# Alternating side banks, eight output products a slot and turned first layers in a fused attention and gated feed-forward kernel

## Chip, cores, metric

The kernel runs on one core of a Trainium2 chip. The metric is device time in microseconds, the median of several executions. PE is TensorE, ACT is ScalarE, DVE is VectorE, POOL is GpSimd, SP is SyncE.

## The reference, cut to what matters

```python
h   = softmax(scale * inducing @ x.T) @ x          # 32 inducing rows, per batch; B = 4, N = 12416, C = 128
a   = softmax(scale * x @ h.T) @ h                 # per token; 49664 tokens in all
g, v = a @ w_gate, a @ w_val                       # 128 -> 1536 each
out = a + sigmoid(a @ w_res) * ((gelu(g) * v) @ w_out)
```

Per token only 32 softmax weights `r` are needed: `a = r @ h`, so `g = r @ (h @ w_gate)`. The first layers `hg = h @ w_gate` and `hv = h @ w_val` are 32 x 1536 per batch; the kernel holds them, halved, in four copies along the partitions. Matmuls go in row-tiled pairs: one takes partitions 0 to 63 and the other 64 to 127, so each sums over two of the copies (a pair of 512 columns takes 0.39 us in the traces).

## The kernel before

The main loop goes by *slots*. A slot computes 1024 columns: a gate pair on PE, Gelu on ACT, a value pair on PE and a product `u` on DVE. Six slots make a *group* of 512 tokens and 12 chunks of 128 features. Everything else is put into a slot's *window*, which is issued after the slot's value pair: the 48 output products of a group (`mms`), two mixes of the group (gate, residual), and work for the next batch. In the traces PE's rows follow the order of the code (slot 5 of the changed kernel: value pair at 745.44, mix at 745.66, products at 745.97).

```python
ps_gv = ... tile_pool(name="psgv", bufs=3, PSUM)    # 3 x 2 banks, gate and value pairs in turn
ps_f  = ... tile_pool(name="psf", bufs=1, PSUM)     # output sums of a group
ps_m  = ... tile_pool(name="psm", bufs=1, PSUM)     # mixes, accumulation, small work
...
def first_layer(b, parts, engs):
    bank = wide_bank()
    ...     # matmuls of 512 columns: all four copies at once, h.T stationary
            act.activation(dst[:, c0:c1], bank[:, o0:o], AC.Copy, bias=0.0, scale=0.5)
...
for gi in range(ngrp):                              # f: first slot of the group
        at(f + 4, lg.gate)                          # mix with hr, then tanh on ACT
        at(f + 6, lg.residual)                      # mix with ha, then a copy on ACT
        for i, n in enumerate((10, 10, 10, 9, 9)):
            at(f + 3 + i, lambda lg=lg, n=n: lg.mms(n))
        at(f + 7, lg.end)                           # DVE: (tanh + 1) * sums; POOL: + residual; store
...
# next batch, per batch: group g, slot p
bg(13 + i, 2, lambda: accumulate(nb, j0, j1, True, True))   # i = 0..4
bg(18, 2, lambda: finish_h(nb)); bg(19, 2, lambda: turn_h(nb))
bg(20, 2, first_layer hg)                           # 1024 columns, one ACT copy
bg(22, 2, first_layer hv); bg(23, 2, first_layer the rest, two copies)
bg(22, 5, lambda: res_layer(nb))
# bursts of exponentials (another ACT table) after slot 2 of groups 12 and 21
```

The trace shows a table load of 1.28 us on ACT before the first exponential of a burst and again before the next Gelu (`ACT_TABLE_LOAD`, 14 in the kernel before, 1283 ns each). Gelus run ahead of the value pairs by a *lead* of up to four slots; a burst sets it to one, and it grows by one in every other group. I number slots by position in the loop: slots 2, 3, 4, 5, then 0 and 1 of the next six, belong to one group's products. Slot 2 has none.

The softmax here doesn't subtract the row's maximum and nothing guards it: scores larger than these inputs give would overflow.

## Time and profile before

| | before |
|---|---|
| median, 4 runs | 865.85 us (864.67 to 866.56) |
| busy DVE, PE, ACT | 92%, 91%, 85% |
| ordinary group, from one closing DVE operation to the next | 7.74 us |
| the two groups after the second burst (22 and 23) | 11.19 + 9.28, 11.31 + 9.28, 8.88 + 9.28 us in batches 1 to 3 |

The closing operation `th<-th,ffn` comes once a group, so differences of its start times are group lengths: the simplest way to compare two kernels of this kind place by place. Groups are counted from 0 in each batch; a *lead-growth* group is one in which the lead grows by one, so that it holds seven Gelus. The lines of the page, the ordinary group and the waits of the first layers stand in the prediction. This is PE in the timeline of an accumulation group, slot 2 (start, length, engine, line; idle time before it in brackets):

```profile
163.94 0.39 PE L289 MATMUL gv<-rt,hv 64*128 64x512 f16 x2
...
164.26 0.25 PE L165 MATMUL ms<-hi,e 128*32 128x128 f16 x4
...
165.52 0.39 PE L289 MATMUL gv<-rt,hv 64*128 64x512 f16 x2 [0.18 <-ACT ge L298]
```

The accumulation starts at 164.26, and even after it PE waits 0.18 us for ACT before it may issue slot 3's value pair: in the empty slot it lies beside a wait. The sums over a stretch in the first batch (us, busy by engine, granted clock, DMA share):

```profile
226.00:234.00 8.00, 5.97 (x91) 3.97 (x88) 7.86 (x12) 6.10 (x8) 1.90 (x1) 0.99 0.18 35
234.00:241.00 7.00, 6.14 (x38) 3.06 (x37) 4.86 (x5) 3.69 (x5) 4.97 (x3) 0.53 0.29 73
```

After eight microseconds in which PE was busy 5.97, the granted clock is on average 0.53 for 7 us (0.50 from 233.8 to 240.6, which I call a half-clock stretch), and DVE works 4.86 of 7.

### The profile page before, as it was taken

The numbers are of one execution on the slowest core, as the hardware profiler recorded it, in microseconds if no ns is written. First come the engines' busy times: TensorE is split into PE (matmuls) and PEld (weight loads), VectorE is DVE, ScalarE is ACT, GpSimd is POOL, SyncE is SP. The second block draws the span as 40 slices with busy tenths as digits, with TensorE's granted clock in tenths as the row PEclk, the third lists the DMA queues.
The fourth block names the chain that finished last, engine by engine and source line by source line (L and its number), as shares of the span: only waits on it lengthen the run. The fifth ranks groups of instructions, "written<-read, shape, count | busy, mean of one in ns | idle before, by whom it ended". The sixth has DMA issues, their size and how long they took to land.

```text
span 863.7 us, 23212 instructions
## 1 busy us (share of the span) xinstructions
PE 789.5 (91%) x9548; PEld 473.8 (55%) x9548; DVE 798.7 (92%) x784; ACT 734.9 (85%) x870; POOL 347.6 (40%) x304
## 2 busy tenths in 40 slices
PE   5889999999889999999988999999988899999997
PEld 4545556555545555656554555565554555555554
DVE  8689999999989999899988999989998999999997
ACT  5588988989878888898978888989888898889885
POOL 2429885112266776112145787411225711111111
PEclk9599999999999999999989999999999999999999
DMA  8337875010147776101034677410114411100111
GB/s 308 108 70 155 199 171 142 27 38 26 38 98 139 185 184 138 41 26 38 26 69 95 165 181 171 104 39 26 38 34 92 101 39 39 38 32 32 38 38 40
DMA packets 114185, 77.04 MB, mean 89 GB/s; under 512 B 92416, under 2 KB 95136, under 8 KB 114080
## 3 DMA queue, kind: packets, MB, share of 16 engines
q1 hardware_dynamic: 111792, 73.14, 33.5%
q10 hardware_dynamic: 2288, 2.43, 1.0%
q8 instruction: 74, 1.21, 0.6%
q14 instruction: 31, 0.25, 0.1%
HBM read 27.87 MB, written 25.43 MB: 62 GB/s over the span
## 4 chain that ended last, share of the span: by engine, by line
PE 68%; DVE 14%; ACT 11%; issue 5%; DMA 1%; POOL 1%; DVEq 0%; POOLq 0%; SPq 0%; ACTq 0%
PE ffn L328 31%; PE gv L289 30%; ACT ge L298 10%; DVE u L305 9%; PE ms L337 4%; DVE lo L116 1%; DVE hi L114 1%; DVE z L242 1%; DVE th L356 1%; ACT hg L215 1%; DMA ge<-in_moe_w_out_dram 1%; POOL wO L417 0%; PE gv L212 0%; DMA rt<-a 0%; DMA xf<-in_x_dram 0%
## 5 line engine op out<-in xcount | busy, mean ns | idle before, releaser
L305 DVE TENSOR_TENSOR u<-ge,gv 128x1024 bf16<-128x1024 f32 x584 | 693.0, 1214 | 48.4 <-PE gv L289 24.2
L298 ACT ACTIVATE ge<-gv 128x1024 f32<-128x1024 f32 x584 | 586.0, 1021 | 88.4 <-PE gv L289 63.6
L328 PE MATMUL ffn<-wO,u 128*128 128x128 bf16 x4656 | 346.8, 221 | 0.6 <-DVE th L356 0.6
L328 PEld LDWEIGHTS <-u 128*128 128x128 bf16 x4656 | 263.7, 98 | 113.9 <-issue 93.0
L359 POOL TENSOR_TENSOR at<-at,th 128x512 f32<-128x512 f32 (+1 forms) x100 | 124.0, 1240 | 428.3 <-ACT ge L298 361.3
L289 PE MATMUL gv<-rt,hv 64*128 64x512 f16 x1152 | 224.1, 380 | 35.6 <-ACT ge L298 22.7
L289 PE MATMUL gv<-rt,hg 64*128 64x512 f16 x1152 | 225.3, 387 | 8.5 <-ACT ge L298 3.1
L289 PEld LDWEIGHTS <-hv 64*128 64x128 bf16 x1200 | 97.0, 94 | 110.5 <-issue 106.3
L289 PEld LDWEIGHTS <-hg 64*128 64x128 bf16 x1200 | 63.1, 93 | 92.1 <-issue 40.9
L256 POOL TENSOR_TENSOR a<-e,z 128x1024 f16<-128x1024 f32 (+2 forms) x50 | 91.2, 1833 | 27.2 <-DMA rt<-a 14.2
L116 POOL TENSOR_TENSOR lo<-xf,hi 128x1024 f16<-128x1024 f32 x36 | 76.8, 2135 | 0.3
L337 PEld LDWEIGHTS <-rt 64*128 64x128 f16 x768 | 57.6, 94 | 30.8 <-issue 3.6
L356 DVE SCALAR_TENSOR_TENSOR th<-th,ffn 128x512 f32<-128x512 f32 (+1 forms) x100 | 66.5, 665 | 1.0 <-PE ffn L328 1.0
L345 ACT ACTIVATE th<-ms 128x512 f32<-128x512 f32 (+1 forms) x100 | 58.0, 580 | 2.4 <-PE ms L337 2.4
L351 ACT ACTIVATE at<-ms 128x512 f32<-128x512 f32 (+1 forms) x100 | 58.0, 580 | 1.9 <-PE ms L337 1.8
L114 POOL CAST hi<-xf 128x1024 f16<-128x1024 f32 x36 | 37.3, 1037 | 29.5 <-DMA xf<-in_x_dram 19.5
L337 PE MATMUL ms<-ha,rt 64*128 64x128 f16 x384 | 36.6, 215 | 1.1 <-DVE hr L225 1.1
L337 PE MATMUL ms<-hr,rt 64*128 64x128 f16 x384 | 37.5, 219 | 0.0
L141 PEld LDWEIGHTS <-xt 128*128 128x128 f16 x768 | 24.3, 99 | 7.0 <-issue 6.4
L132 ACT ACTIVATE xt<-gv 128x1024 f16<-128x1024 f16 x12 | 12.3, 1024 | 13.3 <-PE gv L131 13.3
L131 PE MATMUL gv<-identF,hi 128*128 128x128 f16 x96 | 11.0, 285 | 9.0 <-DVE hi L114 8.8
L235 ACT ACTIVATE e<-gv 128x1024 f32<-128x1024 f32 (+2 forms) x13 | 11.9, 959 | 7.9 <-PE gv L141 7.8
(88 smaller groups left out, 261.3 us busy)
## 6 DMA issues: line engine op xcount, KB each, us to landing
out_dram<-at SPq DMA_DIRECT2D x96, 256.0 KB, 2.0
xf<-in_x_dram SPq DMA_DIRECT2D x42, 512.0 KB, 4.3
ge<-in_x_dram SPq DMA_DIRECT2D x6, 512.0 KB, 6.1
rt<-a SPq DMA_TRANSPOSE x49, 3.1
xt<-hi SPq DMA_TRANSPOSE x36, 3.2
ge<-in_moe_w_gate_dram ACTq DMA_DIRECT2D x1, 512.0 KB, 4.5
ge<-in_moe_w_val_dram ACTq DMA_DIRECT2D x1, 512.0 KB, 5.6
ge<-in_moe_w_out_dram ACTq DMA_DIRECT2D x1, 512.0 KB, 4.5
```

The source lines that it names most:

```text
L114: e_hi.tensor_copy(hi[:, :w, :], xf[:, :w, :])
L116: e_lo.tensor_tensor(lo[:, :w, :P], xf[:, :w, :], hi[:, :w, :], AL.subtract)
L256: po.tensor_tensor(a2[:, :n], ev[:, o:o + n, :].unsqueeze(2).to_broadcast([P, n, Q, M]), z[:, 1, o:o + n].unsqueeze(2).unsqueeze(3).to_bro ...
L289: pe.matmul(v[:, c * tw:(c + 1) * tw], weights[b][r, (c0 + c) * P:(c0 + c + 1) * P], rt[r, :], start=True, stop=True)
L298: act.activation(ge[:, :n], v, AC.Gelu, bias=0.0, scale=1.0)
L305: ve.tensor_tensor(u[:, :n], ge_t.pop((gi, si)), v, AL.mult)
L328: pe.matmul(self.ffn[:, k, :], u_t[self.gi, si][:, o:o + P], wO[:, fc, :], start=first, stop=not self.todo, skip_group_check=True)
L337: pe.matmul(bank[:, k * P:(k + 1) * P], rt_t[self.b, self.k][r, self.j0 + k, :], h[r, :], start=True, stop=True)
L345: act.activation(self.th[:, :self.tw], bank[:, :self.tw], AC.Tanh, bias=0.0, scale=0.5)
L351: act.activation(self.at[:, :self.tw], bank[:, :self.tw], AC.Copy, bias=0.0, scale=1.0)
L356: ve.scalar_tensor_tensor(self.th[:, :tw], self.th[:, :tw], 1.0, self.ffn.rearrange("p k c -> p (k c)")[:, :tw], AL.add, AL.mult)
L359: po.tensor_tensor(self.at[:, :tw], self.at[:, :tw], self.th[:, :tw], AL.add)
```

## The change

Its intent: to spread the products evenly over all six slots (which needs a second bank for the sums, since slot 2 belongs to a time when the last group's sums are still read), to put the mixes at the start of a window, and to make the first layers cheaper for PE's banks and ACT. The diff, cut to its core (schedule conditions, renamed pools and the final drain are cut):

```diff
-    ps_f = ... bufs=1     ps_m = ... bufs=1
+    ps_2 = two pools "ps0", "ps1", bufs=1 each
+    def side_bank(group):
+        return ps_2[group % 2].tile([P, TOK], FP32, name="sb", tag="sb")
     def misc_bank():
-        return ps_m.tile([P, TOK], FP32, name="ms", tag="ms")
+        return side_bank(parity[0] + 1)             # parity: the group of the window
...
+    def first_layer_t(b):                           # 24 matmuls of 32 columns, weights stationary
+        bank = wide_bank()
+        for o, w in ((0, wG), (TOK, wV)):
+            for c in range(FCH):
+                pe.matmul(bank[:, o + c * M:o + (c + 1) * M], w[:, c * P:(c + 1) * P],
+                          ht_t[b][:, 0:M], start=True, stop=True)
+        act.activation(hgt_t[b], ..., AC.Copy, bias=0.0, scale=0.5)   # 768 columns
+    def spread(b, i):                               # POOL copies fourfold, DMA turns it
+        po.tensor_copy(a2, src.unsqueeze(2).to_broadcast([P, n, Q, M]))
+        ... sy.dma_start_transpose(...)
...
-            at(f + 4, lg.gate)
-            at(f + 6, lg.residual)
-            for i, n in enumerate((10, 10, 10, 9, 9)):
-                at(f + 3 + i, lambda lg=lg, n=n: lg.mms(n))
-            at(f + 7, lg.end)
+            for i in range(6):
+                at(f + 2 + i, lambda lg=lg: lg.mms(8))
+            at(f + 5, lg.gate, START)
+            at(f + 6, lg.residual, START)
+            at(f + 7, lg.end, LATE)
...
-                bg(13 + i, 2, ... accumulate ...)
-            bg(18, 2, finish_h)  bg(19, 2, turn_h)
+                bg(13 + i, 3, ... accumulate ..., START)
+            bg(18, 3, finish_h, START)  bg(19, 3, turn_h, START)
+            bg(20, 3, first_layer_t, START)
+            for i in range(3):
+                bg(20, 5 + i, lambda i=i: spread(nb, i))
-            bg(20, 2, first_layer hg)  bg(22, 2, hv)  bg(23, 2, the rest)
-            bg(22, 5, lambda: res_layer(nb))
+            bg(23, 3, lambda: res_layer(nb), START)
```

The output buffers `u` go from 8 to 7. Both mixes of a group now use the other group's bank, one after the other.

More of the change, by code (lines that the diff above doesn't have):

```diff
@@ L71 @@
     p_ge = ctx.enter_context(tc.tile_pool(name="gelu", bufs=6))
-    p_u = ctx.enter_context(tc.tile_pool(name="up", bufs=8))
+    p_u = ctx.enter_context(tc.tile_pool(name="up", bufs=7))
     p_fin = ctx.enter_context(tc.tile_pool(name="fin", bufs=2))
     ps_gv = ctx.enter_context(tc.tile_pool(name="psgv", bufs=3, space=bass.MemoryType.PSUM))
-    ps_f = ctx.enter_context(tc.tile_pool(name="psf", bufs=1, space=bass.MemoryType.PSUM))
-    ps_m = ctx.enter_context(tc.tile_pool(name="psm", bufs=1, space=bass.MemoryType.PSUM))
+    ps_2 = [ctx.enter_context(tc.tile_pool(name=f"ps{i}", bufs=1, space=bass.MemoryType.PSUM))
+            for i in range(2)]
     ctx.enter_context(tc.manual_schedule())
+    parity = [0]
+    def side_bank(group):
+        return ps_2[group % 2].tile([P, TOK], FP32, name="sb", tag="sb")
     def misc_bank():
-        return ps_m.tile([P, TOK], FP32, name="ms", tag="ms")
+        return side_bank(parity[0] + 1)
     def wide_bank():
@@ L217, in first_layer @@
                 ve.tensor_scalar(dst[:, c0:c1], bank[:, o0:o], 0.5, None, op0=AL.mult)
+    hgt_t = {}
+    def first_layer_t(b):
[4 more added lines that the diff above has]
+                          ht_t[b][:, 0:M], start=True, stop=True)
+        hgt_t[b] = p_h.tile([P, 2, FCH * M], BF16, name="hgt", tag="hgt", bufs=1)
+        act.activation(hgt_t[b], bank.rearrange("p (s n) -> p s n", s=2)[:, :, :FCH * M],
+                       AC.Copy, bias=0.0, scale=0.5)
+    def spread(b, i):
+        n = 2 * FCH // 3
+        src = hgt_t[b].rearrange("p s (c m) -> p (s c) m", m=M)[:, i * n:(i + 1) * n, :]
+        a2 = p_sm.tile([P, PRE, Q, M], BF16, name="a2", tag="a2")
+        po.tensor_copy(a2, src.unsqueeze(2).to_broadcast([P, n, Q, M]))
+        for dst, c0, c1 in ((hg_t[b], 0, FCH), (hv_t[b], FCH, 2 * FCH)):
+            lo, hi = max(c0, i * n), min(c1, (i + 1) * n)
+            if lo < hi:
+                sy.dma_start_transpose(
+                    dst.rearrange("p (c f) -> p c f", f=P)[:, lo - c0:hi - c0, :],
+                    a2[:, lo - i * n:hi - i * n].rearrange("p c q m -> p (c q m)"))
     def res_layer(b):
@@ L323, in mms @@
                 if first:
-                    self.ffn = ps_f.tile([P, TOK // P, P], FP32, name="ffn", tag="ffn")
+                    self.ffn = side_bank(self.gi).rearrange("p (k c) -> p k c", c=P)
                 si, c = divmod(fc, per)
@@ L333, in mix @@
         def mix(self, h):
-            bank = misc_bank()
+            bank = side_bank(self.gi + 1)
             r = slice(0, 2 * M)
@@ L451 @@
         norm_b(0, j0, j1, exp_b(0, j0, j1))
-    warm = ps_f.tile([P, TOK // P, P], FP32, name="ffn", tag="ffn")
+    warm = side_bank(0)
     for i in range(10):
-        pe.matmul(warm.rearrange("p k c -> p (k c)"), wG[:, :P], wG[:, :TOK],
-                  start=True, stop=True)
+        pe.matmul(warm, wG[:, :P], wG[:, :TOK], start=True, stop=True)
     flat = [(gi, si) for gi in range(ngrp) for si in range(len(groups[gi][4]))]
@@ L469, with at @@
     LEAD = 4
-    def at(i, f):
-        windows.setdefault(i, []).append(f)
+    START, MIDDLE, END, LATE = range(4)
+    def at(i, f, where=MIDDLE):
+        windows.setdefault(i, []).append((where, f))
     for gi in range(ngrp):
@@ L477 @@
         if len(groups[gi][4]) == 6:
-            at(f + 4, lg.gate)
-            at(f + 6, lg.residual)
-            for i, n in enumerate((10, 10, 10, 9, 9)):
-                at(f + 3 + i, lambda lg=lg, n=n: lg.mms(n))
-            at(f + 7, lg.end)
-        else:
-            at(f + 1, lg.gate)
-            at(f + 3, lg.residual)
+            for i in range(6):
[3 more added lines that the diff above has]
+            at(f + 7, lg.end, LATE)
+        else:
+            at(f + 2, lg.gate, START)
             at(f + 3, lambda lg=lg: lg.mms(len(lg.todo)))
-            at(f + 3, lg.end)
+            at(f + 3, lg.residual, START)
+            at(f + 3, lg.end, LATE)
     def plan(b):
@@ L491, in plan, with bg @@
         i0 = first[b * gpb]
-        def bg(g, p, f):
-            at(i0 + 6 * g + p, f)
+        def bg(g, p, f, where=END):
+            at(i0 + 6 * g + p, f, where)
         if b == 0:
@@ L510, in plan @@
             for i, (j0, j1) in enumerate(zip(cuts, cuts[1:])):
-                bg(13 + i, 2, lambda j0=j0, j1=j1: accumulate(nb, j0, j1, True, True))
-            bg(18, 2, lambda: finish_h(nb))
-            bg(19, 2, lambda: turn_h(nb))
+                bg(13 + i, 3, lambda j0=j0, j1=j1: accumulate(nb, j0, j1, True, True), START)
+            bg(18, 3, lambda: finish_h(nb), START)
+            bg(19, 3, lambda: turn_h(nb), START)
+            bg(20, 3, lambda: first_layer_t(nb), START)
+            for i in range(3):
+                bg(20, 5 + i, lambda i=i: spread(nb, i))
             e2s = []
@@ L522, in plan @@
                 bg(21, 3 + i, lambda: norm_b(nb, *e2s.pop(0)))
-            bg(20, 2, lambda: first_layer(nb, [(hg_t[nb], wG, 0, cw)], [act]))
-            bg(22, 2, lambda: first_layer(nb, [(hv_t[nb], wV, 0, cw)], [act]))
-            bg(23, 2, lambda: first_layer(
-                nb, [(hg_t[nb], wG, cw, F), (hv_t[nb], wV, cw, F)], [act, act]))
-            bg(22, 5, lambda: res_layer(nb))
+            bg(23, 3, lambda: res_layer(nb), START)
             for i in range(ntile):
                 j = 6 * 21 + 5 + (5 * i) // 2
-                at(i0 + j, lambda i=i: weights_b(nb, i))
+                at(i0 + j, lambda i=i: weights_b(nb, i), END)
     for b in range(B):
@@ L546, in window_next @@
     def window_next():
-        for f in windows.pop(sent["w"], []):
+        i = sent["w"]
+        if i < nflat:
+            parity[0] = flat[i][0]
+        for _, f in sorted(windows.pop(i, []), key=lambda e: e[0]):
             f()
@@ L575 @@
     assert not bursts
-    for i in sorted(windows):
-        for f in windows[i]:
-            f()
+    while windows:
+        window_next()
 _INS = ['x', 'inducing', 'moe_w_gate', 'moe_w_val', 'moe_w_out', 'moe_w_res']
```

## The prediction

> **What bounds the kernel now.** I read the engine table first, then the costliest groups, then the timeline of one ordinary group late in the kernel, then the places where VectorE (DVE) waits. From the page:
>
> ```profile
> PE 789.5 (91%) x9548; PEld 473.8 (55%) x9548; DVE 798.7 (92%) x784; ACT 734.9 (85%) x870; POOL 347.6 (40%) x304
> ...
> L305 DVE TENSOR_TENSOR u<-ge,gv 128x1024 bf16<-128x1024 f32 x584 | 693.0, 1214 | 48.4 <-PE gv L289 24.2
> L298 ACT ACTIVATE ge<-gv 128x1024 f32<-128x1024 f32 x584 | 586.0, 1021 | 88.4 <-PE gv L289 63.6
> ```
>
> Three engines are near full, so the balance inside a slot decides. A slot is one gate pair, one value pair, a Gelu and a DVE product `u`; six slots make a group of 512 tokens. DVE looks saturated, but its rows hide small waits. These are DVE rows of the timeline (start, length, group):
>
> ```profile
> 146.06 2.35 DVE L305 TENSOR_TENSOR u<-ge,gv 128x1024 bf16<-128x1024 f32 x2
> ...
> 743.07 0.68 DVE L356 SCALAR_TENSOR_TENSOR th<-th,ffn 128x512 f32<-128x512 f32 x1
> 743.67 7.23 DVE L305 TENSOR_TENSOR u<-ge,gv 128x1024 bf16<-128x1024 f32 x6
> ...
> 750.81 0.68 DVE L356 SCALAR_TENSOR_TENSOR th<-th,ffn 128x512 f32<-128x512 f32 x1
> ```
>
> Two `u` with nothing between take 2.35 us, so one follows another after 2.35 - 1.22 = 1.13 us. Six would take 5 x 1.13 + 1.22 = 6.87; they take 7.23. So each ordinary group loses about 0.36 us that no idle column shows. Its period is 750.81 - 743.07 = 7.74 us, against a DVE floor of 6 x 1.13 + 0.60 = 7.38 (0.60 is 743.67 - 743.07). The next rows, of PE and ACT in the same group, show where the loss is:
>
> ```profile
> 745.34 1.02 ACT L298 ACTIVATE ge<-gv 128x1024 f32<-128x1024 f32 x1 [0.60 <-PE gv L289]
> 745.61 0.73 PE L328 MATMUL ffn<-wO,u 128*128 128x128 bf16 x10
> 746.26 0.59 ACT L345 ACTIVATE th<-ms 128x512 f32<-128x512 f32 x1
> 746.28 0.39 PE L289 MATMUL gv<-rt,hg 64*128 64x512 f16 x2
> ...
> 747.82 0.39 PE L289 MATMUL gv<-rt,hv 64*128 64x512 f16 x2
> 748.03 0.38 PE L337 MATMUL ms<-ha,rt 64*128 64x128 f16 x4
> 748.35 0.68 PE L328 MATMUL ffn<-wO,u 128*128 128x128 bf16 x9
> ...
> 748.95 0.39 PE L289 MATMUL gv<-rt,hg 64*128 64x512 f16 x2
> 749.18 0.38 PE L289 MATMUL gv<-rt,hv 64*128 64x512 f16 x2
> ```
>
> PE from one value pair to the next, 747.82 to 749.18, needs 1.36 us, more than DVE's 1.13; the following `u` starts 0.49 after the second. The other part comes from ACT: tanh stands between two Gelus, the value pair at 747.82 waits for the bank that the second one reads. Slot 2, by contrast, has no output products, and there PE waits 0.27 us for ACT.
>
> The larger waits are in the second half of each of the first three batches, where the next batch's first layer is made:
>
> ```profile
> 237.13 1.22 DVE L305 TENSOR_TENSOR u<-ge,gv 128x1024 bf16<-128x1024 f32 x1 [0.71 <-PE gv L289]
> 239.29 1.22 DVE L305 TENSOR_TENSOR u<-ge,gv 128x1024 bf16<-128x1024 f32 x1 [0.93 <-PE gv L289]
> ...
> 249.02 1.22 DVE L305 TENSOR_TENSOR u<-ge,gv 128x1024 bf16<-128x1024 f32 x1 [1.37 <-ACT hv L215]
> ```
>
> [...] from 234 to 241 us the granted clock is 0.53 here, after the scores' burst, and that is in the waits of 0.71 and 0.93.
>
> **The change part by part.** *Products.* PE lengths from the rows: value pair to first product 0.31 (749.18 to 749.49), with a mix between 0.53 (747.82 to 748.35); ten products to the next gate pair 0.67, nine 0.60, so eight about 0.55; gate to value pair 0.22. Before: slots 3 and 5 take 0.31 + 0.67 + 0.22 = 1.20, slot 4 (gate mix) 1.42, slot 0 (residual mix) 1.36, slot 1 1.13. After: 1.08 each, and 1.30 in the two mix slots, 5 and 0. All plain slots fall under DVE's 1.13. But the two mix slots now follow each other and share one bank, so the residual mix waits until tanh has read the gate mix.
>
> After, steady state: a value pair can run no earlier than about 0.6 before its `u` starts, since its bank goes `u` end, gate pair, Gelu, value pair (0.06 + 0.45 + 1.02 + 0.06 + 0.49 past a `u` end, against 2 x 1.13). That is 0.1 to 0.2 of slack. Slots 5 and 0 use 2 x (1.30 - 1.13) = 0.34 of it. The mix's wait for tanh: Gelu of slot 5 starts about 0.45 after its gate pair, tanh 0.92 later, its end with the release 0.65 later, 2.0 in all; PE itself reaches the mix 0.22 + 1.30 + 0.22 = 1.75 after the gate pair, or 1.9 where the value pair waits for a Gelu. So another 0.05 to 0.2. Estimate of the group's loss: 0.34 - 0.15 + 0.1 = 0.29, against 0.36. Gain 0.07 a group; some 50 ordinary groups: -4 us.
>
> *Groups where the lead of Gelus grows* (nine; 8.63 us each, with waits of 0.35 and 0.20): the 0.35 is two Gelus in one slot and stays; the PE chain from slot 3 to slot 1 shrinks from 1.20 + 1.42 + 1.20 + 1.36 = 5.18 to 1.08 x 2 + 1.30 x 2 + 0.1 = 4.86. -0.3 each, -3 us.
>
> *First layers.* Removed per batch: six 512-column matmuls, three wide banks, two ACT copies of 1.02 and two of 0.60, 3.2 us of ACT. Added: 24 matmuls of 32 columns (32 scores take 0.9 us, so 0.7), one wide bank, one copy of 768 columns [...], three POOL copies of some 1 to 1.9 us and four transposes, hidden: POOL is 40% busy and the result is wanted some 25 us later. The stretch from 220 to 246 keeps its 0.53 at group 20[...]. The two groups after the second burst take 245.79 - 234.61 = 11.2 and 255.07 - 245.79 = 9.3, and without the copies should take about 8.1 each: -4.3 in the first and second batches, -2 in the third (no slow clock there). Where the clock drops again, some 2.5 of it stay; I put that at 0.6 for each of the two, and 0.3 for the third. Expected: -4.3 x 2 - 2.0 + 2.5 x 1.5 = -6.8, say -7.
>
> *What it costs.* The gate mix falls at the end of a burst of exponentials, so tanh comes just before the table is loaded back: +0.4 in each of six bursts, about a third of it hidden under sums on DVE, +1.5. Accumulation moves from the empty slot 2 to slot 3, which has products now: about 0.7 us of PE, covered by the DVE copy and slack, 0 to +0.2 in 15 groups; finish and turn of `h` likewise. +1.5 together.
>
> Sum: -4 - 3 - 7 + 3 = -11 us, to 854. I lean 2 us further, as the change closes the empty slot and my slack terms round against it: 852.
>
> **The rivals.** *The floor is reached:* the mixes don't bind, and ordinary groups fall to 7.4: 0.35 x 50 = 17 us, twice as much in the disturbed ones' share, about 832. For it: plain slots fit. Against it: two mix slots of 1.30 in a row do not. *The tanh wait binds:* the shared bank adds 0.2 more a group than I count, 7.9 us, and the gain of the first layers is eaten: 860 to 865. For it: 2.0 against 1.75 is a real wait; against it: DVE's closing operation of 0.60 gives PE time once a group, so nothing accumulates. *DMA or POOL become the bound:* [...] Nothing waits for them in time; 0.
>
> **Range and chances.** The ordinary groups carry +-0.12 each, so +-8 with the alike ones; the clock and first layers +-4. I take 840 to 862. 2% faster is below 848.0: 0.33. Slower by 2% needs a wait of 0.3 in every group that I don't see: 0.02.
>
> **What would show it.** Right: the ordinary group's period 7.6 to 7.7; PE waiting for tanh before the residual mix, 0.05 to 0.3; the waits for `hv` and the one of 1.37 gone; ACT busy about 7 to 8 us less; DVE busy unchanged; lead-growth groups at 8.3. Wrong: a period of 7.4 to 7.5 (mixes hidden), or 7.8 and more (shared bank binds), or a third slow-clock stretch.

The copy's estimate was a part of "ACT busy about 7 to 8 us less"; from the copies of 1.02 us for 1024 columns and 0.60 for 512 it comes to about 0.81 (an estimate), and in the changed kernel it took 0.81. What the trace of the kernel before shows: POOL takes 1.04 us for a cast and 1.90 for a product of 128x1024, which "1 to 1.9" matches (the three copies took 1.04 each); the table load before the Gelu after a burst takes 1.28 (228.40 in the first batch).

## The result, and the profile after

The changed kernel takes 857.93 us (857.57 to 858.21, four runs) against 865.85: ratio 0.991, interval 0.9893 to 0.9927.

From the page of the changed kernel:

```profile
PE 795.1 (93%) x9602; PEld 479.1 (56%) x9602; DVE 796.7 (93%) x784; ACT 734.1 (86%) x861; POOL 356.9 (42%) x313
...
L338 DVE TENSOR_TENSOR u<-ge,gv 128x1024 bf16<-128x1024 f32 x584 | 691.1, 1213 | 41.8 <-PE gv L322 26.0
L331 ACT ACTIVATE ge<-gv 128x1024 f32<-128x1024 f32 x584 | 591.7, 1023 | 79.3 <-PE gv L322 67.0
```

ACT has nine instructions fewer but is as busy. The Gelus are as long as before (1023 against 1021 ns), yet count for 591.7 against 586.0 us: busy time counts overlapping tails once (before, 584 of 1021 ns would be 596.3), and fewer Gelus now follow each other without a gap (58 pairs overlap in place of 98). So the three columns hardly tell what happened. Group lengths do (trace against trace, -7.75 us at the last closing operation):

| where | sum of the differences |
|---|---|
| up to the first closing operation | -1.7 |
| 12 groups at or after a batch's start where the lead of Gelus grows | -3.4 |
| three groups with the first burst | +2.0 |
| 15 groups with an accumulation and three with the finish of `h` (13 to 18) | +6.5 |
| groups 19 to 21 | +0.3 |
| groups 22 and 23 | -13.2 (-5.1, -5.3, -2.8) |
| the rest, most of them ordinary groups of 7.76 against 7.74 | +1.0 |
| last group | +0.8 |

The first row is not the change's doing as far as is known: that point lies between 55.0 and 61.1 us in the fourteen traces, with half-clock stretches at other places before it (the last one ends at 52.9 before and at 39.6 here).

Groups 22 and 23 in the first batch, the closing operations and the stretch that was slow before:

```profile
235.65 0.68 DVE L389 SCALAR_TENSOR_TENSOR th<-th,sb 128x512 f32<-128x512 f32 x1
...
243.16 0.68 DVE L389 SCALAR_TENSOR_TENSOR th<-th,sb 128x512 f32<-128x512 f32 x1
...
250.99 0.68 DVE L389 SCALAR_TENSOR_TENSOR th<-th,sb 128x512 f32<-128x512 f32 x1
```

```profile
234.00:241.00 7.00, 5.90 (x63) 3.43 (x62) 6.96 (x10) 5.02 (x6) 4.53 (x3) 1.00 0.32 80
```

7.51 and 7.83 us in place of 11.19 and 9.28; the clock is full and DVE busy 6.96 of 7.

An ordinary group, PE, ACT and DVE:

```profile
742.03 0.68 DVE L389 SCALAR_TENSOR_TENSOR th<-th,sb 128x512 f32<-128x512 f32 x1
...
744.37 2.16 ACT L331 ACTIVATE ge<-gv 128x1024 f32<-128x1024 f32 x2 [0.35 <-PE gv L322]
...
745.44 0.39 PE L322 MATMUL gv<-rt,hv 64*128 64x512 f16 x2
...
746.43 0.59 ACT L378 ACTIVATE th<-sb 128x512 f32<-128x512 f32 x1
...
746.75 0.38 PE L322 MATMUL gv<-rt,hv 64*128 64x512 f16 x2
...
747.07 0.38 PE L370 MATMUL sb<-ha,rt 64*128 64x128 f16 x4
...
748.16 0.38 PE L322 MATMUL gv<-rt,hv 64*128 64x512 f16 x2
...
749.79 0.68 DVE L389 SCALAR_TENSOR_TENSOR th<-th,sb 128x512 f32<-128x512 f32 x1
```

The empty slot is gone and PE's plain slots are short, but the two mix slots follow each other: 745.44 to 746.75 is 1.31, 746.75 to 748.16 is 1.41, the latter with 0.10 of waiting for tanh (a mix else starts 0.215 after its value pair, here 0.32; tanh ends at 747.02). The group is 7.76 long, where it was 7.74.

And slot 3 of an accumulation group:

```profile
164.40 0.39 PE L322 MATMUL gv<-rt,hv 64*128 64x512 f16 x2 [0.25 <-ACT ge L331]
164.72 0.25 PE L172 MATMUL sb<-hi,e 128*32 128x128 f16 x4
...
165.41 0.62 PE L361 MATMUL sb<-wO,u 128*128 128x128 bf16 x8
...
166.19 0.38 PE L322 MATMUL gv<-rt,hv 64*128 64x512 f16 x2
```

Value pair to value pair is now 1.79 us, 0.7 of it the accumulation, and PE waits for nothing within it; the Gelu after it waits 1.13 us for PE.

### The profile page after: what moved, and what is told of

It is laid out like the page before. It is cut to its first block, busy times and chain, and to the rows that moved or that the text cites. A ratio compares the mean times of both kernels' runs of the same rounds, so it can differ in the third digit from the quotient of the medians.

```text
span 855.8 us, 23356 instructions
## 1 busy us (share of the span) xinstructions
PE 795.1 (93%) x9602; PEld 479.1 (56%) x9602; DVE 796.7 (93%) x784; ACT 734.1 (86%) x861; POOL 356.9 (42%) x313
## 4 chain that ended last, share of the span: by engine, by line
PE 52%; DVE 25%; issue 11%; ACT 8%; DMA 1%; POOL 1%; DVEq 0%; ACTq 0%; POOLq 0%; SPq 0%
PE gv L322 26%; DVE u L338 19%; PE sb L361 19%; ACT ge L331 6%; PE sb L370 5%; DVE lo L123 2%; DVE th L389 1%; DVE z L275 1%; DVE hi L121 1%; PE sb L172 1%; ACT at L384 1%; ACT th L378 1%; DMA ge<-in_moe_w_out_dram 1%; PE sb L174 0%; POOL wO L450 0%
## 5 line engine op out<-in xcount | busy, mean ns | idle before, releaser
L331 ACT ACTIVATE ge<-gv 128x1024 f32<-128x1024 f32 x584 | 591.7, 1023 | 79.3 <-PE gv L322 67.0
L361 PE MATMUL sb<-wO,u 128*128 128x128 bf16 x4656 | 360.5, 220 | 0.1
L322 PEld LDWEIGHTS <-hv 64*128 64x128 bf16 x1200 | 99.5, 94 | 103.0 <-issue 88.6
L389 DVE SCALAR_TENSOR_TENSOR th<-th,sb 128x512 f32<-128x512 f32 (+1 forms) x100 | 66.4, 664 | 1.8 <-PE sb L361 1.8
L378 ACT ACTIVATE th<-sb 128x512 f32<-128x512 f32 (+1 forms) x100 | 57.9, 579 | 8.8 <-PE sb L370 8.6
L384 ACT ACTIVATE at<-sb 128x512 f32<-128x512 f32 (+1 forms) x100 | 58.0, 580 | 0.8 <-PE sb L370 0.8
L370 PE MATMUL sb<-ha,rt 64*128 64x128 f16 x384 | 36.5, 214 | 0.2
L370 PE MATMUL sb<-hr,rt 64*128 64x128 f16 x384 | 36.6, 215 | 0.0
L139 ACT ACTIVATE xt<-gv 128x1024 f16<-128x1024 f16 x12 | 12.3, 1024 | 13.4 <-PE gv L138 13.3
```

The lines of the kernel that those rows point to most:

```text
L322: pe.matmul(v[:, c * tw:(c + 1) * tw], weights[b][r, (c0 + c) * P:(c0 + c + 1) * P], rt[r, :], start=True, stop=True)
L331: act.activation(ge[:, :n], v, AC.Gelu, bias=0.0, scale=1.0)
L361: pe.matmul(self.ffn[:, k, :], u_t[self.gi, si][:, o:o + P], wO[:, fc, :], start=first, stop=not self.todo, skip_group_check=True)
L370: pe.matmul(bank[:, k * P:(k + 1) * P], rt_t[self.b, self.k][r, self.j0 + k, :], h[r, :], start=True, stop=True)
L378: act.activation(self.th[:, :self.tw], bank[:, :self.tw], AC.Tanh, bias=0.0, scale=0.5)
L384: act.activation(self.at[:, :self.tw], bank[:, :self.tw], AC.Copy, bias=0.0, scale=1.0)
```

## The experiments

All gave correct results. Times are medians; "before" was run in the same rounds and took 864.7 to 865.0. Runs of different rounds are compared by their ratios to before.

| run | us | ratio to before |
|---|---|---|
| t_only | 853.94 | 0.9879 (0.9863 to 0.9894) |
| s_only | 861.87 | 0.9963 (0.9948 to 0.9977) |
| gate4 | 864.38 | 1.0002 (0.9985 to 1.0019) |
| acc2 | 860.02 | 0.9943 (0.9928 to 0.9957) |
| prod66 | 856.0 | 0.9896 (0.987 to 0.9921) |
| split10 | 875.01 | 1.0107 (1.0086 to 1.0128) |
| t_p | 848.24 | 0.9799 (0.9775 to 0.9824) |
| t_res | 852.68 | 0.9851 (0.9826 to 0.9876) |
| t_p_res | 847.02 | 0.9797 (0.9779 to 0.9816) |
| acc3 | 876.76 | 1.0147 (1.0117 to 1.0176) |
| res_only | 864.43 | 0.9995 (0.9981 to 1.0009) |
| res_end | 860.06 | 0.9943 (0.9924 to 0.9962) |

### The change's two halves

**t_only**: the kernel before plus the turned first layers.

```diff
+    first_layer_t, spread as in the change; "up" bufs 8 -> 7
-            bg(20, 2, first_layer hg)  bg(22, 2, hv)  bg(23, 2, the rest)
+            bg(20, 2, lambda: first_layer_t(nb))  bg(20, 5 + i, spread(nb, i))
```

> The kernel before with the turned first layers alone (and one output buffer fewer, 7 for 8, to make room). Theory (the turned first layers are the whole gain, and the new order of the slots gives it partly back): the groups 22 and 23 after the second burst fall from 11.2 and 9.3 us to about 7.6 to 8.1 in the first two batches, no stretch at half clock there, all else as before: 14 us less than before, 851 to 853, which is 6 us faster than the changed kernel. Rival (the gain needs the new order too, since the first layer was moved to a slot with room): no more than 7 us less than before, 858 or more.

Measured 853.94: 10.8 us less than before, faster than the whole change (0.9879 against 0.991; the intervals just touch), though less than I expected. Groups 22 and 23 are 8.54 + 8.08, 8.36 + 8.08, 8.36 + 8.09. A stretch of 3.4 us at half clock remains in the first batch. (Its profiled execution, the slowest of four, had a mean granted clock of 0.938, the others 0.984 to 0.986; two ordinary groups in its trace take 7.77 us each, against 7.74 before and in t_res.)

**s_only**: the changed kernel with the old first layers.

```diff
-            bg(20, 3, first_layer_t, START) ... spread
+            bg(20, 2, first_layer hg)  bg(22, 2, hv)  bg(23, 2, the rest)
```

> The changed kernel with the old first layers put back (three wide banks and four ACT copies in groups 20, 22, 23), all of the new order kept. Theory: the order alone costs about 6 us, so 870 to 874, slower than before by 0.7%. Rival (the two parts help each other, or the order gains by itself): 866 or less.

Measured 861.87, 3 us *less* than before: my theory fell. The order alone does cost what the table shows (accumulation groups 8.15 to 9.10, first bursts 10.67), but it also takes groups 22 and 23 to 7.76 + 8.96 in all three batches, with no stretch at half clock. In the third batch, which has no half-clock stretch in any of the four traces (t_only's execution at a mean clock of 0.938), the two groups take 18.16 before, 16.45 with the turned layers, 16.72 with the order, 15.34 with both: there the halves nearly add (1.71 + 1.44 against 2.82). In the first two batches, with a half-clock stretch in it, group 22 before was some 2.3 us longer (11.19 against 8.88), and either half saves most of that, so there they overlap. The overlap of the two runs, 10.8 + 2.9 - 7.9 = 5.8 us, is about that: 2.3 + 2.4 of half clock counted twice, and 0.3 in each of three batches.

**res_only**: of the order, just the residual layer moved.

```diff
-            bg(22, 5, lambda: res_layer(nb))
+            bg(23, 2, lambda: res_layer(nb))
```

> The kernel before with only the residual layer moved, to slot 2 of group 23. Theory (its bank was half of what made group 22 long, and the changed kernel got that half by moving it, not by the turned layers): group 22 of the third batch falls from 8.88 to 8.1 to 8.4; in all 1 to 3 us less than before, more where the half-clock stretches shorten. Rival: no change in group 22 of the third batch.

864.43, no gain in time. The profiled execution fell to half clock after the burst in the first and third batches (10.65 and 10.85), so the group that I named says nothing; the second batch, at full clock, has 8.35 against 8.88 of a full-clock batch before. That is the size expected, but on one group, and group 23 beside it grew to 9.45 from 9.28.

**t_res**: the same move on top of the turned layers.

```diff
+    first_layer_t, spread as in t_only
-            bg(22, 5, lambda: res_layer(nb))
+            bg(23, 2, lambda: res_layer(nb))
```

> The kernel before with the turned first layers, and the residual layer of the next batch at slot 2 of group 23 in place of slot 5 of group 22, where the mix of the next slot waited for its bank. Theory (that wait is what keeps group 22 at 8.4 to 8.5 us here against 7.5 in the changed kernel): group 22 falls by 0.6 to 0.9 in each of three batches, 1.5 to 2.5 us less than the turned first layers alone. Rival (group 22 needs the new order of products): no change in group 22.

852.68, ratio 0.9851 against 0.9879 from other rounds. Group 22 is 7.61 where the clock was full (second batch), 0.75 less than t_only's 8.36 there, and 8.26 and 8.41 where a half-clock stretch fell on it. So the wait for the bank is real (before, the mix waits 0.36 us for the residual layer at 243.02), and without it group 22 is within 0.1 of the changed kernel's 7.51 without any new order of products.

### The accumulation

**acc2**: in the changed kernel, the accumulation after slot 2's products.

```diff
-                bg(13 + i, 3, ... accumulate ..., START)
+                bg(13 + i, 2, ... accumulate ..., END)
```

> The changed kernel with the accumulation of the next batch back in slot 2, after that slot's products, in place of the start of slot 3. Theory (in slot 3 its 0.7 us stands between two value pairs where no slack is): the five groups with it fall from 8.16 and 9.03 us to about 7.9 and 8.7, 4 us less than the changed kernel in all. Rival (it costs the same in any slot that has products, only the empty slot hid it): within 1 us of the changed kernel.

860.02, no better (0.3% worse by the ratios, so beyond the rival's 1 us too), and the rival's reason holds: an accumulation pair (one group with the lead growing, one without) takes 8.80 + 8.52 = 17.3 against 9.03 + 8.16 = 17.2. Slot 2 as such is not the cure.

**acc3**: in the kernel before, one move.

```diff
-                bg(13 + i, 2, ... accumulate ...)
+                bg(13 + i, 3, ... accumulate ...)
```

> The kernel before with one thing moved: the accumulation of the next batch in slot 3, after that slot's products, in place of the empty slot 2; it keeps its own bank. Theory (the place is what cost the changed kernel about 0.35 us in each accumulation group: in the empty slot PE only waits for ACT, in slot 3 it does not): a pair of accumulation groups goes from 8.62 + 7.86 = 16.5 to 17.0 to 17.4, in all 4 to 6 us more than before. Rival (the shared side bank and the adjacent mixes cost it, not the place): 16.5 stays, within 1 us of before.

```profile
167.84 0.68 DVE L356 SCALAR_TENSOR_TENSOR th<-th,ffn 128x512 f32<-128x512 f32 x1
177.34 0.68 DVE L356 SCALAR_TENSOR_TENSOR th<-th,ffn 128x512 f32<-128x512 f32 x1
186.15 0.68 DVE L356 SCALAR_TENSOR_TENSOR th<-th,ffn 128x512 f32<-128x512 f32 x1
```

876.76. The pair takes 9.50 + 8.81 = 18.3 us, against 16.5 before and 17.2 in the changed kernel. These are before's and then the changed kernel's closing operations of the same groups:

```profile
163.81 0.68 DVE L356 SCALAR_TENSOR_TENSOR th<-th,ffn 128x512 f32<-128x512 f32 x1
172.43 0.68 DVE L356 SCALAR_TENSOR_TENSOR th<-th,ffn 128x512 f32<-128x512 f32 x1
180.29 0.68 DVE L356 SCALAR_TENSOR_TENSOR th<-th,ffn 128x512 f32<-128x512 f32 x1
```

```profile
162.75 0.68 DVE L389 SCALAR_TENSOR_TENSOR th<-th,sb 128x512 f32<-128x512 f32 x1
171.77 0.68 DVE L389 SCALAR_TENSOR_TENSOR th<-th,sb 128x512 f32<-128x512 f32 x1
179.93 0.68 DVE L389 SCALAR_TENSOR_TENSOR th<-th,sb 128x512 f32<-128x512 f32 x1
```

With its own bank and the old mixes, the place alone costs, and more than I expected (that slot has ten products). Together with acc2: what hid the accumulation was an *empty* slot. The evenness of the change sold that room. The finish of `h`, which the change moved as well (+0.47 in group 18), was not moved alone; its cause is taken to be the same, not shown.

### The products and the mixes

**gate4**: in the changed kernel, the gate mix one slot earlier.

```diff
-            at(f + 5, lg.gate, START)
+            at(f + 4, lg.gate, START)
```

> The changed kernel with the gate mix at the start of slot 4 in place of slot 5: the mixes no longer follow each other and the residual mix has a slot for tanh to be done. Theory (two mix slots in a row and the residual mix's wait for tanh make the 0.37 us lost per ordinary group): the ordinary group falls from 7.76 to about 7.70, the group with the first burst from 10.67 to about 10.1 (tanh is no longer after the last exponentials): 5 to 7 us less than the changed kernel, about 851. Rival (the loss is the chain over ACT, gate pair, Gelu, tanh, Gelu, value pair, wherever the mix stands): ordinary groups stay at 7.74 to 7.78, 855 or more.

864.38, worse than the changed kernel (1.0002 against 0.991), and the ordinary group stays (the line between is a gate pair):

```profile
747.66 0.68 DVE L389 SCALAR_TENSOR_TENSOR th<-th,sb 128x512 f32<-128x512 f32 x1
...
749.53 0.39 PE L322 MATMUL gv<-rt,hg 64*128 64x512 f16 x2 [0.18 <-DVE u L338]
...
755.42 0.68 DVE L389 SCALAR_TENSOR_TENSOR th<-th,sb 128x512 f32<-128x512 f32 x1
```

7.76. The first burst came back to 9.98, as said, so the 0.68 there is tanh after the last exponential. But accumulation pairs rose to 9.08 + 8.65, since the gate mix one slot after the accumulation needs the same bank (it waits 0.42 for DVE's copy at 173.26), and groups 19 and 23 by 0.73 and 0.52. Adjacent mixes are not what holds the ordinary group. Following its starts in this trace gives a loop over all three engines: DVE's closing operation, the next `u` (+0.60), the gate pair that waits for that `u`'s bank, the line above (+1.27), its Gelu (+0.48), tanh (+0.92), the next Gelu (+0.48), value pair of slot 0 (+1.08), value pair of slot 1 (+1.30), its `u` (+0.49), the closing operation (+1.14): 7.76. The same walk in the changed kernel, from the value pair of slot 1, goes through DVE for four steps (value pair to `u` 0.49, `u` to the closing operation 1.14, next `u` 0.60, next `u` 1.13), then gate pair 0.13, Gelu 0.48, value pair 1.07, the two mix slots 1.31 and 1.41: 7.76 too. The 1.41 holds the 0.10 of waiting for tanh, so slot 5's own 1.31 has that much room and what binds there is ACT: Gelu, Gelu, tanh, then the mix. Three wide banks tie all three engines into loops of nearly the same length.

**prod66**: in the changed kernel, two products fewer in each mix slot.

```diff
-            for i in range(6):
-                at(f + 2 + i, lambda lg=lg: lg.mms(8))
+            for i, n in enumerate((8, 8, 8, 6, 6, 12)):     # slots 2, 3, 4, 5, 0, 1
+                at(f + 2 + i, lambda lg=lg, n=n: lg.mms(n))
```

> The changed kernel with products 8, 8, 8, 6, 6, 12 in slots 2, 3, 4, 5, 0, 1 in place of eight each: two fewer in each of the two mix slots, four more in the slot that ends with DVE's closing operation. Theory (what holds the ordinary group at 7.76 us is a loop in which PE's length of slots 5 and 0 is a part: value pair of slot 5, mix, products, value pair of slot 0, wait for tanh, mix, products, value pair of slot 1): slot 0's part is 0.11 us shorter and slot 5's is hidden by tanh, so 7.65 to 7.72, 3 to 5 us less than the changed kernel. Rival (ACT's part of the loop binds alone): 7.76 stays, within 1 us.

```profile
740.44 0.68 DVE L389 SCALAR_TENSOR_TENSOR th<-th,sb 128x512 f32<-128x512 f32 x1
748.09 0.68 DVE L389 SCALAR_TENSOR_TENSOR th<-th,sb 128x512 f32<-128x512 f32 x1
```

7.65: the loop's PE part is real, and shortening it by 0.11 gives 0.11. In all less than expected, 0.9896 against 0.991, since lead-growth and accumulation groups got up to 0.11 and group 23 0.24 longer.

**split10**: the old split in the changed kernel.

```diff
-            for i in range(6):
-                at(f + 2 + i, lambda lg=lg: lg.mms(8))
+            for i, n in enumerate((0, 10, 10, 10, 9, 9)):
+                at(f + 2 + i, lambda lg=lg, n=n: lg.mms(n))
```

> The changed kernel with the old split of the products, none in slot 2 and then 10, 10, 10, 9, 9. Theory (eight products a slot gain a little in the groups where the lead grows, and cost in the groups with an accumulation, since slot 2 is no longer empty for PE to catch up): ordinary groups 7.78 to 7.85, lead-growth groups back from 8.34 to about 8.6, accumulation groups from 8.16 and 9.03 to about 8.0 and 8.8; in all within 4 us of the changed kernel, rather slower. Rival (eight a slot is what costs): 3 us or more faster than the changed kernel.

875.01, 17 us slower than the changed kernel, far more than the 4 expected. Ordinary groups are 7.82, as worked out (3 us in all), and lead-growth groups 8.68 (some 4), but the groups 13 to 18 rose too, by 0.25 to 0.34 each (5.5), to pairs of 9.36 + 8.45, where I expected them to fall, and groups 22 and 23 by 2.5 in all. Its first closing operation also came 2.0 later in the trace, after a start with other half-clock stretches. Eight a slot is thus right *for* this placing of mixes and accumulation. This kernel has an empty slot 2 but accumulates in slot 3, so it says nothing against the empty slot as a place.

**res_end**: in the changed kernel, the residual mix after slot 0's products.

```diff
-            at(f + 6, lg.residual, START)
+            at(f + 6, lg.residual, END)
```

> The changed kernel with the residual mix after the eight products of slot 0 in place of ahead of them: PE's length of the slot is the same, but the mix no longer waits for tanh to have read the shared bank (0.10 us per ordinary group in the trace). Theory: ordinary group from 7.76 to 7.65 to 7.70, 3 to 5 us less than the changed kernel. Rival (the wait lies beside ACT's own work, and ACT holds the loop): 7.74 to 7.78.

860.06, worse. Ordinary groups go back and forth between 7.69 and 7.76, 7.72 on average: 0.04 of the 0.10 was gained, less than the theory and more than the rival said. The wait for tanh is gone, but the mix comes later, so ACT's copy and the Gelu behind it do too. The time was lost elsewhere: in this trace the groups 13 to 18 take 1.3 us more than in the changed kernel's, groups 19 to 21 0.7, first bursts 0.6, the last group 0.7.

**t_p**: the kernel before with the turned layers and another split.

```diff
+    first_layer_t, spread as in t_only
-        for i, n in enumerate((10, 10, 10, 9, 9)):
+        for i, n in enumerate((8, 10, 12, 8, 10)):          # slots 3, 4, 5, 0, 1
```

> The kernel before with the turned first layers, and products 8, 10, 12, 8, 10 in slots 3, 4, 5, 0, 1 in place of 10, 10, 10, 9, 9. Theory (same loop: the slots 3 and 0 shorter by 0.11 and 0.06, slot 5 has room since tanh holds it anyway): ordinary group from 7.75 to about 7.68, 3 to 4 us less than the kernel with the turned first layers alone. Rival (ACT binds alone): within 1 us of it.

```profile
741.82 0.68 DVE L382 SCALAR_TENSOR_TENSOR th<-th,ffn 128x512 f32<-128x512 f32 x1
749.49 0.68 DVE L382 SCALAR_TENSOR_TENSOR th<-th,ffn 128x512 f32<-128x512 f32 x1
```

7.67, as worked out from the loop; 848.24 in all, ratio 0.9799 against t_only's 0.9879 of other rounds.

**t_p_res**: t_p and the moved residual layer.

```diff
+    first_layer_t, spread as in t_only
-        for i, n in enumerate((10, 10, 10, 9, 9)):
+        for i, n in enumerate((8, 10, 12, 8, 10)):
-            bg(22, 5, lambda: res_layer(nb))
+            bg(23, 2, lambda: res_layer(nb))
```

> All that helped so far on the kernel before: turned first layers, products 8, 10, 12, 8, 10 in slots 3 to 1, residual layer at slot 2 of group 23. Theory (the three add): 1.5 to 2.5 us below the version without the moved residual layer (848.2), 845.5 to 847, ratio to before 0.977 to 0.979. Rival (the moved layer and the split share one wait): 848 stays.

847.02, ratio 0.9797: the best here, 1.1% under the changed kernel by the ratios to before (0.9797 over 0.991). Whether it is 2% under the kernel before is open, its interval holds both. Against t_p the ratios are the same, so that the moved layer adds is shown only by group 22 in its trace (7.55, 7.55, 7.55 against 8.30, 8.83, 8.30), not by the times.

### The half clock

In the traces' clock records, the groups after the second burst had a half-clock stretch in 12 of 24 batches of the eight kernels with an empty slot 2 (before, t_only, split10, t_p, t_res, t_p_res, acc3, res_only), and in 1 of 18 of the six with products there (the changed kernel, s_only, gate4, acc2, prod66, res_end). The kernel before has them at 233.8 to 240.6 and 442.0 to 448.8, the changed kernel none there. Each is one execution, and t_p_res has none in spite of its empty slot. The mean granted clock says that the traced ones are typical: before has a median of 0.979 in its 29 executions of the experiments' rounds, the changed kernel 0.986 to 0.988 in four. The difference of 0.008 over some 860 us is 7 us of clock, or two half-clock stretches of 6.8 us (an estimate; 6.8 is the one of the kernel before from 233.8 to 240.6). The medians of the kernels with an empty slot and turned first layers (0.984 to 0.987) hardly differ from those of the kernels with slot 2 filled (0.985 to 0.988). That filling slot 2 keeps the clock up is likely, not shown.

## Why the prediction was right, and where not

The time, 857.9, lies in the range, the forecast of "within 2%" held, and the gain is 7.9 us of the 14 (865.85 to 852). Its terms, though, missed in both directions:

- *What bounds the kernel* was right: every ordinary group loses about 0.36 us that no idle column shows, from PE's mix slots and tanh between Gelus (prod66 and t_p shortened PE's part and the group with it); after the change 7.76 - 7.38 = 0.38 remains.
- *Steady state, "Estimate of the group's loss: 0.29"*: wrong. The parts were right (1.31 and 1.41 for the mix slots, a wait of 0.10 for tanh), the slack was mis-sized. I took 0.15; in the trace slot 5's value pair starts 0.58 before its `u` (746.02, three steps of 1.13 after the group's first at 742.63), 0.09 more than the 0.49 it needs; the Gelu before it starts 0.48 rather than 0.45 after its gate pair. Gain 0 in place of 4 us. prod66 and t_p show that the same arithmetic is good to 0.02 us a group once the loop is walked around to its own start, not only from one value pair.
- *Lead growth, "-0.3 each, -3 us"*: right: 8.34 for 8.62, -3.4 with the group after each batch's end.
- *First layers, -7*: the mechanism was right, the size half. The waits for `hv` and the 1.37 are gone. I expected "about 8.1 each" and a clock that still drops (an estimate); the two groups took 7.51 and 7.83 and the clock stayed full (1.00 from 234 to 241). And not all of it is the first layers': t_only and s_only show that the new order, with the moved residual layer, brings 1.1 to 1.4 of the 2.8 us that the third batch gained. How much of the half clock's end is due to which part stays open.
- *Bursts, +1.5*: +2.0 in the first bursts, +0.2 in the second ones. Right in sum; that sums on DVE hide it there was argued, not tested.
- *Accumulation, "covered by the DVE copy and slack, 0 to +0.2 in 15 groups"*: the step that failed. +0.25 to +0.48 in 18 groups, 6.5 us in place of the 1.5 put down for it, finish and turn together. acc3 shows that the place is the cost in before's order, and acc2 that slot 2 is no cure once it has products: the copy gives DVE 0.34, but PE needs 0.7 between two value pairs, and the Gelu behind them comes late too (1.13 of waiting).
- *ACT busy 7 to 8 us less*: wrong as a sign, 0.8: nine copies went, but busy time counts overlap once.
- *The rivals*: the floor was not reached; the tanh wait is there, and res_end, which removes it, gained 0.04 of its 0.10 in an ordinary group; after the first closing operation no wait of PE, ACT or DVE is put down to DMA or POOL in the trace, and the new transposes landed 3.2 and 3.4 us after their issue.

So the number was near by luck: errors cancelled. First layers gained about 6 us more than I said, part of it half-clock time, and accumulation and ordinary groups lost 5 us each against what I said.

## What to carry to other kernels

Where several engines run near full and a few rotating banks tie them, walk one full loop of starts back to itself and count which lengths are in it; a length that is not in the loop (a wait beside another engine's work) is worth nothing. An uneven schedule can be holding room for rare work: before evening it out, see what lies in its empty slot. And compare group lengths place by place, since a change of 1% can be -13 and +8.

## What the traces show of the hardware

- Granted clock. In the kernel before it was 0.50 for 6.8 us (233.8 to 240.6) after a stretch of 8 us in which PE's longest wait was 1.43 us and PE was busy 5.97 us. What makes it drop is not shown. One profiled execution (t_only) had a mean of 0.938, where the other three of that kernel had 0.984 to 0.986.
- Output products. Each has its own weight load, and they run at 56 to 57 ns (ten in 0.73 us, with the last one's 0.22).
- Busy time. Records of neighbouring DVE operations overlap by 0.09 us (1.22 long, 1.13 apart), so waits up to 0.09 do not show as idle and longer ones show too small; and ACT's busy time stayed at 734 us while nine instructions and some 7 us of work went (3 x 3.2 us of old copies out, 3 x 0.81 in).
- The delay from a gate pair's start to a Gelu that waits for it is 0.43 us in most groups and 0.48 in others (742.56 to 742.99 and 743.89 to 744.37 in the changed kernel). The 0.05 is a third of the slack that the prediction reckoned with; what decides between the two is not shown, ACT having idled before both (0.27 and 0.35).
